# GpSimd makes the third shifted pattern of VectorE's packs in a gated attention kernel; 127 packs instead of 120

## The chip, the cores and the metric

The kernel runs on one core of a Trainium2 chip. The core has five engines with a queue each: TensorE (PE, with its weight loads shown as PEld), VectorE (DVE), ScalarE (ACT), GpSimd (POOL) and SyncE (SP, which here only starts DMAs). A queue is worked in order; semaphores tie the queues together. The metric is the device time of one execution in microseconds, as the median of several runs.

## What is computed

Two attention branches read the same `x` (2,048 tokens of 512) and are mixed by a gate of one number per token:

```
g = sigmoid((x * gate_w).sum(-1))
a: qkv = x @ A_wqkv;  p = softmax(q k^T * 16**-0.5);  a = (p v) @ A_wo      32 heads of 16
b: qkv = x @ B_wqkv;  pq = q w_phi;  pk = k w_phi
   phi_q = [softmax(pq), softmax(-pq)];  phi_k = [softmax(pk), softmax(-pk)]
   kv = phi_k^T v;  z = sum phi_k;  b = (phi_q kv / (phi_q z + 1e-6)) @ B_wo
out = g * a + (1 - g) * b
```

Nearly all the work is the softmax of branch a: 32 heads with 2,048 x 2,048 scores each.

## The kernel before

**Tiles.** A *unit* is the score block of one head, 128 keys against 512 queries. Four heads side by side in TensorE's 32-row tiles make a *pack*; 16 packs (all the keys) make a *group* of four heads and 512 queries, and 32 groups make the 512 packs, or 2,048 units.

**Two ways through the exponential.** Most units go to ScalarE: `_qk` writes two or three units' scores to PSUM, alternately, in a ring of five banks, `_exp` (L1019) turns them into bf16 in the tile `ET`, and `_pv` (through `_values`, L1085) multiplies a pack by the values and adds into the group's bank. Each exponential waits for its scores; each score call waits for the last exponential but one. The packs listed in `AWAY`, five bits per group for the packs 1, 4, 7, 10 and 13, go to VectorE instead. `_vector_bits` writes the scores of one unit at a time into one of the three other PSUM banks (L971 in `_scores`), and VectorE scales and shifts them into 16-bit integers (L911, tile `va`) whose bits, read as bf16, are a rough power of two. `_vector_terms` makes three copies of them, shifted by 30, 62 and 95 (`SHIFTS`, L927, tile `vp`). The four patterns, the unshifted one among them, are multiplied by the values (for the two last ones by values scaled by 0.75, tile `vc`) and added up on TensorE in `_pv_terms`; their sum comes close to the exponential. Up to two packs of a group make a *turn*: the eight bits instructions fill one half of `va`, and each term instruction covers the whole turn, 4,096 elements in a partition, or 2,048 where the turn has one pack. There are two halves of `va`, used in turns, and one `vp` tile for each shift.

**After a group.** `_norm` turns the bank, divides by the sum, multiplies by the gate and sends the result through DMAs into `onTA`; `_out` multiplies by `A_wo`. Branch b (`_b_quad`, `_b_kv`, `_b_num`, `_b_out`) is spread over the run in between: its exponentials are ScalarE's (L1258), most of its element work is VectorE's (L1229 to L1286). POOL fills constants at the start and does little else.

**Order.** Nothing is ordered by hand. `Plan.op` records each operation with its engine, a cost in microseconds, what it reads and writes, and a due time in packs; `SHIFT` moves the due times of tagged operations. `Plan.order` then runs through the operations, always taking for the engine that is free first what is ready and due first, with the booked costs, and so writes down each engine's queue. `emit` puts these queues and their semaphore waits into the program. TensorE's queue also gets *fillers*: value matmuls with zero weights (`_fill`, L1092), where its recent use falls under a share.

Of the kernel before, what the change touches and what calls it, by code (L numbers as in the profile page):

```python
# [6 lines left out]
ACT = mybir.ActivationFunctionType  # L7
ALU = mybir.AluOpType
# [7 lines left out]
QCH = 512  # L16
# [27 lines left out]
class Op:  # L44
    def __init__(self, eng, fn, cost, name, prio, rel, kind, lat):
        self.eng, self.fn, self.cost, self.name = eng, fn, cost, name
        self.prio, self.rel, self.kind, self.lat = prio, rel, kind, lat
        self.deps = []
        self.users = []
        self.left = 0  # L50
        self.need = False
        self.acquire = None
        self.release = None
        self.sem = None
        self.start = self.end = None
        self.commit = None
        self.array = 0.0
        self.filler = 0
        self.slack = None
        self.fits = True  # L60
        self.pad = False
        self.tiles = []
        self.filled = 0
        self.tag = None

# [38 lines left out]
class Plan:  # L104
# [4 lines left out]
    LAT = {"PE": 0.20, "ACT": 0.17, "DVE": 0.12, "POOL": 0.12, "SP": 2.2}  # L109
# [3 lines left out]
    EVICT = 30.0  # L113
    COST, NEAR = 30.0, 0.05
# [11 lines left out]
    def op(self, eng, fn, cost, reads=(), writes=(), deps=(), name="", prio=0.0, rel=-99, kind="full",  # L126
           acquire=None, release=None, lat=None, array=None):
        o = Op(eng, fn, cost, name, prio, rel, kind, self.LAT[eng] if lat is None else lat)
        found = {}
# [36 lines left out]
    def order(self):  # L166
# [15 lines left out]
        recent = []  # L182
        queues = {e: [] for e in self.ENGS}
        left = len(self.ops)
        seq = {id(o): i for i, o in enumerate(self.ops)}
        while left:
            best = None
            for e in self.ENGS:
                found, limit = [], 1e9
                for o in avail[e]:  # L190
# [4 lines left out]
                    for d in o.deps:  # L195
                        r = d.end + (d.lat if d.eng != e or e == "SP" else 0.0 if e == "PE" else self.CHAIN)
                        if r > t:
                            t = r
                    if o.acquire is not None:
# [34 lines left out]
            o = pick[1]  # L234
# [27 lines left out]
            free[e] = array.seq if e == "PE" else o.end  # L262
            queues[e].append(o)
# [113 lines left out]
class _Kernel:  # L377
# [10 lines left out]
    TURN = 2.2  # L388
    LAST, RAMP, PART = 8.0, 48, 24
# [335 lines left out]
    def _gate(self):  # L725
# [44 lines left out]
    AWAY = (15, 5, 27, 26, 20, 27, 14, 28, 30, 13, 23, 31, 14, 14, 30, 31, 29, 14, 23, 7, 31, 27, 23, 23, 30, 31, 11, 27, 11, 31, 23, 31)  # L770

    SHIFT = (
        ("k5", -3), ("k4", -10), ("v1", -6.5), ("p30", -4.5), ("p13", 7), ("p22", 8.5), ("q1", 3.5), ("w0", -10),
        ("p18", -11.5), ("b1", -7.5), ("v2", -5), ("x1", -5), ("v4", 6), ("p21", -3), ("p2", 0.5), ("k1", -6),
        ("p26", 10.5), ("k6", 6), ("b4", -3), ("p0", 1), ("g1", -6), ("p38", -5), ("p31", 1), ("d0", -3.5), ("p34",
        -1), ("p32", -6), ("v9", 6.5), ("e2", 13.5), ("p47", 6), ("p75", 2.5), ("b93", 11.5), ("b77", 6.5), ("b90",
        8.5), ("a0", 7.5), ("p89", -3.5), ("g4", 10.5), ("x90", -5.5), ("p104", -12), ("p98", 2), ("e4", 2), ("q5",
        6.5), ("x138", -0.5), ("p126", 1.5), ("x141", 13.5), ("p137", -1), ("t125", 7), ("p113", 12), ("b138",
        -4.5), ("a4", -6), ("b154", -14), ("p112", 10), ("p152", 11), ("p144", -2.5), ("p171", 4), ("p159", -10),
        ("p168", 11.5), ("p163", -0.5), ("p162", -12.5), ("x177", -14), ("g11", 4.5), ("x199", 0.5), ("p184", 8),  # L780
        ("d12", -0.5), ("p210", -3.5), ("p254", -12), ("p240", -11), ("p245", -7.5), ("p236", -2), ("g14", 4.5),
        ("b257", -3), ("t257", -4), ("b279", 1), ("p256", 2), ("p255", -5.5), ("p270", 4), ("p258", -14), ("p284",
        -12.5), ("x257", 2.5), ("b301", -8.5), ("p286", 12), ("p287", 14), ("p291", -10), ("b311", -1.5), ("p307",
        10.5), ("p296", -10.5), ("p294", -4), ("p315", 11.5), ("p306", -13.5), ("t289", 4), ("p300", -0.5), ("p302",
        -0.5), ("o0", 7), ("p304", -4.5), ("p297", 4), ("p293", 11.5), ("b327", 8.5), ("h5", 6), ("n5", 3), ("p318",
        7), ("p332", 2), ("p331", 7), ("p338", 4), ("p341", 7.5), ("p363", 12.5), ("h8", 4), ("x372", 6), ("p367",
        -8), ("p386", -5), ("p396", 1), ("b397", 7), ("f3", 6), ("b404", -2), ("p409", -8), ("p392", 0.5), ("p400",
        14), ("p421", -1.5), ("b420", -2), ("o8", -5.5), ("p403", -2), ("p405", -1), ("p423", 13.5), ("p438", 1.5),
        ("h14", 8), ("p432", -1.5), ("h12", -6.5), ("x445", -1), ("g27", 8.5), ("b471", 12), ("x449", -1.5),
        ("p456", -2.5), ("t449", -10.5), ("p464", 14), ("p476", -6.5), ("p467", 3.5), ("t481", 7), ("p478", -5),  # L790
        ("p470", 3.5), ("p482", -2), ("x487", -4), ("o15", 3), ("p496", -1), ("g30", -1), ("x509", -4), ("g31", 12),
        ("p501", 12), ("p511", 0.5), ("v3", -9), ("t7", 4), ("p8", 12.5), ("e1", -1), ("v8", 8.5), ("p50", -4),
        ("p82", -6), ("d4", -3.5), ("p107", -8), ("d8", -11), ("p133", 8), ("p146", 11), ("q6", 12.5), ("b177",
        -14), ("p217", 2), ("g13", 3), ("p224", 2), ("x244", 9), ("h3", 2.5), ("b295", 13), ("g17", 11.5), ("b308",
        0.5), ("x308", 9), ("b337", -9), ("p344", 3), ("h4", 3.5), ("o7", 13), ("x407", 1), ("p399", -4), ("b407",
        -8), ("x420", 9), ("b452", 12.5), ("p443", 8), ("o13", -4.5), ("p502", 3), ("p14", 12), ("p3", 9), ("t1",
        -12.5), ("p25", 12), ("t17", -12), ("b33", 7), ("b7", -1.5), ("b17", -4), ("gate", -1.5), ("e0", 13.5),
        ("e3", 7.5), ("p44", 2.5), ("x42", 4.5), ("p85", 7.5), ("p73", -3), ("x93", -2.5), ("p78", 13.5), ("p95",
        7.5), ("p123", -14), ("b212", -6.5), ("e12", 1), ("p198", -7), ("x180", -6), ("p178", 8.5), ("e14", 5),
        ("p211", 8), ("p222", 6.5), ("p238", -5.5), ("p230", 6), ("p283", -11), ("p281", 13.5), ("x321", 3),  # L800
        ("t327", 0.5), ("p319", -1.5), ("x340", -1), ("p389", 11.5), ("n8", -6.5), ("b401", -1), ("t407", -12),
        ("q14", 1), ("b426", 2.5), ("x426", 4.5), ("p447", -6.5), ("h15", -7), ("p462", -0.5), ("x465", -9.5),
        ("b481", 10.5), ("t477", 6.5), ("n14", 4.5), ("x477", -7), ("b503", -3.5), ("p510", -2.5), ("x481", 1),
        ("p5", 9), ("p19", 13), ("v0", 3), ("k3", -8.5), ("w1", -1), ("b10", 4), ("p35", -1), ("p37", -5.5), ("p43",
        12.5), ("p69", 1), ("p67", 0.5), ("b84", -3), ("p96", 10), ("b103", 5), ("b119", 5), ("p131", -10.5),
        ("t177", -0.5), ("b180", 8.5), ("b186", -4), ("x189", 2), ("q7", 8.5), ("x212", -2), ("b244", -5), ("p235",
        -11.5), ("b282", -7.5), ("x301", 6.5), ("p299", -0.5), ("p290", 9.5), ("p312", 1), ("g19", 11.5), ("x337",
        -3), ("g20", -5), ("g22", 12), ("x388", 10.5), ("b394", -10.5), ("p384", -1), ("x394", 3.5), ("p395", -8),
        ("b388", -1), ("o9", 6), ("p437", -6.5), ("p451", -6), ("p473", -3), ("x493", 0.5), ("g29", 1.5), ("b500",
        -5), ("b487", 11.5), ("p492", -2.5), ("p504", 8), ("b468", 9.5), ("x500", 8), ("b23", 7.5), ("x10", -10),  # L810
        ("x17", -3), ("b45", -0.5), ("q2", 0.5), ("p488", -4), ("n7", 2), ("p446", 8), ("p450", 11.5), ("t433",
        -3.5), ("p57", 11), ("p56", -9), ("p63", 7), ("b81", 7.5), ("n11", 1.5), ("b449", 7), ("n13", 7), ("x497",
        -10), ("t417", 8), ("p110", 4), ("p102", 9.5), ("p114", 11.5), ("p143", -8.5), ("p134", -6.5), ("p142", -4),
        ("p153", -7), ("t145", -0.5), ("p412", -0.5), ("x145", 7.5), ("g28", 10.5), ("n15", 10.5), ("x154", -10),
        ("o12", -5), ("p494", -1.5), ("x173", 10), ("x218", 7.5), ("g12", 6), ("x228", -4.5), ("x231", -1.5),
        ("p239", 5), ("h2", -8), ("x247", -12), ("x263", -0.5), ("n2", 9), ("g15", -11), ("f1", 5.5), ("q10", 1),
        ("p316", 5.5), ("o2", -9.5), ("p313", 10.5), ("p310", 8.5), ("p309", -2), ("x324", -8.5), ("p325", 9),
        ("p320", -5), ("p345", 2), ("p339", 12), ("h6", 12.5), ("p379", 8.5), ("p378", -2), ("p382", 11), ("p53",
        4.5), ("p39", -2), ("x58", -7), ("g3", -3.5), ("k12", 1), ("q3", 4.5), ("p83", -12.5), ("p79", 6.5),
        ("x103", -2), ("p108", 1), ("p124", 2), ("p129", -1.5), ("p139", -3), ("e9", 14), ("p158", -8), ("p169",  # L820
        -1), ("p166", -2.5), ("p176", -13.5), ("p188", 1.5), ("p204", -8), ("p190", -4), ("p191", 6), ("x196", 2),
# [673 lines left out]
```

## Time and profile before

The median of three runs is 757.48 us (757.35 to 757.73). The profiled execution has a span of 755.7 us from its first to its last instruction.

| engine | busy us | share of the span | instructions |
|---|---|---|---|
| ScalarE (ACT) | 740.9 | 98% | 647 |
| VectorE (DVE) | 723.2 | 96% | 1126 |
| TensorE (PE) | 719.6 | 95% | 7307 |
| GpSimd (POOL) | 7.8 | 1% | 17 |

Busy is the time in which an engine has at least one instruction under way, so that neighbours which overlap in the record are not counted twice; a group's mean duration can therefore be longer than its share of the busy time. The idle time behind a group's bar is that of the engine just before these instructions, with what ended it. The granted TensorE clock is 1.000 over the whole span.

### The profile page before, as it was taken

Reading aid. Unit: us, or ns where it says so; the run is one execution under the profiler, and the core shown is the slowest. Engines: PE = TensorE matmul, PEld = TensorE weight load, DVE = VectorE, ACT = ScalarE, POOL = GpSimd, SP = SyncE. Lnnn points to the kernel's source line nnn. Section 1 sums busy time; section 2 is a strip of 40 time slices with the busy share of each in tenths; the row PEclk is TensorE's granted clock in tenths of the full one; section 3 lists DMA queues with packets and bytes.
Section 4 is the critical chain, followed back from the end, with each engine's and each line's share of the span. In section 5 each row is a group of like instructions: output and inputs, shape, how many; then the busy total and the mean of one; then the engine's idle time right before and its main releaser. Section 6 shows DMA issues by size and latency. Waiting matters only on the chain.

```text
span 755.7 us, 17044 instructions
## 1 busy us (share of the span) xinstructions
PE 719.6 (95%) x7307; PEld 232.0 (31%) x7368; DVE 723.2 (96%) x1126; ACT 740.9 (98%) x647; POOL 7.8 (1%) x17
## 2 busy tenths in 40 slices
PE   8999999999999999999999999999999999999997
PEld 3334233333322322223222323223222223322332
DVE  6989899979999999999999999999999999999997
ACT  5999999999999999999999999999999999999996
POOL 3000000000000000000000000000000000000000
PEclk9999999999999999999999999999999999999999
DMA  9300001000000010100103111310112201131010
GB/s 212 131 5 6 10 8 17 8 3 14 8 8 15 2 14 9 15 9 3 21 13 57 24 15 37 73 27 8 23 29 47 38 17 29 29 73 28 11 27 29
DMA packets 90027, 21.78 MB, mean 29 GB/s; under 512 B 82912, under 2 KB 89440, under 8 KB 89952
## 3 DMA queue, kind: packets, MB, share of 16 engines
q1 hardware_dynamic: 88224, 20.17, 13.2%
q8 instruction: 57, 0.93, 0.5%
q10 hardware_dynamic: 1728, 0.52, 0.3%
q14 instruction: 18, 0.15, 0.1%
HBM read 4.21 MB, written 2.10 MB: 8 GB/s over the span
## 4 chain that ended last, share of the span: by engine, by line
ACT 93%; PE 5%; DVE 1%; DMA 1%; issue 0%; DVEq 0%
ACT ET L1019 89%; ACT bq L1258 4%; PE ps L971 1%; PE ps L1085 1%; DMA xT<-in_A_x_dram 1%; PE ps L714 1%; PE ps L1388 0%; PE ps L1434 0%; PE ps L641 0%; DVE va L911 0%; PE ps L992 0%; DVE kT L664 0%; DVE qT L697 0%; ACT xT L1444 0%; DVE V L720 0%
## 5 line engine op out<-in xcount | busy, mean ns | idle before, releaser
L1019 ACT ACTIVATE ET<-ps 128x1536 bf16<-128x1536 f32 x627 | 713.3, 1383 | 5.6 <-PE ps L971 5.3
L971 PE MATMUL ps<-qT,kT 32*128 32x512 bf16 x2048 | 314.6, 384 | 14.2 <-ACT ET L1019 7.3
L911 DVE TENSOR_SCALAR va<-ps 128x512 uint16<-128x512 f32 x480 | 311.5, 680 | 12.0 <-PE ps L971 9.5
L927 DVE TENSOR_SCALAR vp<-va 128x4096 uint16<-128x4096 uint16 (+1 forms) x204 | 219.2, 1086 | 0.9 <-PE ps L1085 0.6
L971 PEld LDWEIGHTS ps<-qT,kT 32*128 32x128 bf16 x2048 | 82.2, 91 | 260.6 <-ACT ET L1019 158.0
L1085 PE MATMUL ps<-ET,V 128*32 128x512 bf16 x1568 | 150.2, 386 | 0.4 <-DVE T L1106 0.2
L1085 PE MATMUL ps<-vp,vc 128*32 128x512 bf16 x960 | 86.4, 384 | 1.0 <-DVE vp L927 1.0
L1092 PE MATMUL ps<-kT,zero 128*32 128x512 bf16 x744 | 63.3, 384 | 0.0
L1085 PEld LDWEIGHTS ps<-ET,V 128*32 128x32 bf16 x1568 | 39.2, 95 | 65.0 <-issue 50.4
L641 PE MATMUL ps<-WB,xT 128*128 128x512 bf16 x164 | 50.0, 383 | 5.6 <-issue 3.0
L1085 PE MATMUL ps<-vp,V 128*32 128x512 bf16 x480 | 46.9, 384 | 0.5 <-DVE vp L927 0.5
L1085 PE MATMUL ps<-va,V 128*32 128x512 bf16 x480 | 47.3, 384 | 0.0
L641 PE MATMUL ps<-xT,WA 128*128 128x512 bf16 (+1 forms) x114 | 33.2, 375 | 2.8 <-issue 1.6
L1085 PEld LDWEIGHTS ps<-vp,vc 128*32 128x32 bf16 x960 | 23.1, 95 | 37.1 <-issue 19.5
L1258 ACT ACTIVATE bq<-bq 128x2048 bf16<-128x2048 bf16 x16 | 32.3, 2034 | 0.0
L1229 DVE CAST bq<-ps 128x512 bf16<-128x512 f32 x32 | 21.7, 682 | 4.1 <-PE ps L641 4.0
L1106 DVE STREAM_TRANSPOSE T<-ps 128x512 f32<-128x512 f32 x32 | 22.6, 707 | 2.2 <-PE ps L1085 2.2
L1092 PEld LDWEIGHTS ps<-kT,zero 128*32 128x32 bf16 x744 | 16.0, 94 | 25.1 <-issue 22.2
L714 PE MATMUL ps<-WA,xT 128*128 128x128 bf16 x256 | 21.1, 220 | 0.8 <-DVE V L720 0.3
L1256 DVE TENSOR_TENSOR bq<-bq,btree 128x2048 bf16<-128x2048 bf16 x16 | 19.4, 1210 | 0.0
L641 PEld LDWEIGHTS ps<-WB,xT 128*128 128x128 bf16 x192 | 11.9, 97 | 23.6 <-issue 13.4
L714 PEld LDWEIGHTS ps<-WA,xT 128*128 128x128 bf16 x256 | 15.1, 98 | 10.4 <-issue 6.9
(83 smaller groups left out, 330.9 us busy)
## 6 DMA issues: line engine op xcount, KB each, us to landing
turned<-T SPq DMA_DIRECT2D x240, 8.0 KB, 1.8
qT<-qs SPq DMA_DIRECT2D x120, 16.0 KB, 1.8
WB<-in_B_wqkv_dram SPq DMA_DIRECT2D x1, 1536.0 KB, 8.0
out_dram<-WB SPq DMA_DIRECT2D x12, 128.0 KB, 1.7
WA<-in_A_wqkv_dram SPq DMA_DIRECT2D x3, 384.0 KB, 5.5
WoA<-in_A_wo_dram SPq DMA_DIRECT2D x1, 512.0 KB, 9.0
WoB<-in_B_wo_dram SPq DMA_DIRECT2D x1, 512.0 KB, 9.6
WA<-in_A_wqkv_dram ACTq DMA_DIRECT2D x3, 128.0 KB, 4.1
```

Source lines behind the costliest of these rows:

```text
L641: ins = e.matmul(self._bank(job)[:, 0:n], lhs(c), rhs(c), start=(c == 0), stop=(c == 3))
L714: ins = e.matmul(self._bank(job)[:, P * tt:P * tt + P], self.xT[:, c, QCH * j + TOK * tt:QCH * j + TOK * tt + TOK], self.WA[:, 2, c, P * c ...
L911: parts.append(op("DVE", lambda e, j=j, job=job: e.tensor_scalar(self.va[:, pair, side, j, :], self._bank(job), SCALE * LOG2E * 128.0, (12 ...
L927: self.plan.op("DVE", lambda e, k=k, shift=shift: e.tensor_scalar(flat(self.vp[:, k]), flat(self.va[:, pair]), float(shift), None, op0=ALU ...
L971: return e.matmul(out, self.kT[32 * i:32 * i + 32, cp, kt * TOK:(kt + 1) * TOK], self.qT[32 * i:32 * i + 32, s, :], start=True, stop=True, ...
L1019: o = plan.op("ACT", lambda e: e.activation(self.ET[:, a % NS:a % NS + n, :], self.ps[:, self._ring(a):self._ring(a) + n, :], ACT.Exp, sca ...
L1085: ins = e.matmul(self._bank(ot)[32 * i:32 * i + 32, :], V[:, v0:v0 + 32], tile(), start=(kt == 0), stop=(kt == self.NT - 1), tile_position ...
L1092: ins = e.matmul(self._bank(ot)[32 * i:32 * i + 32, :], self.zero[:], self.kT[:, 0, 0:QCH], start=False, stop=False, tile_position=(0, 32 ...
L1106: op("DVE", lambda e: e.transpose(T1[:, side].rearrange("p b s -> p (b s)"), src()), 0.635, deps=last, writes=[b_T1[side]], name="n_t1", p ...
L1229: [lambda e, b, k=k: e.tensor_copy(bq[:, k].rearrange("p (g s v) -> p g s v", g=8, s=2)[:, :, 0, :], b.rearrange("p (g v) -> p g v", g=8))],
L1256: run("b_sub", two(2048), lambda e, out=out, t=t: e.tensor_tensor(out, p, spread(t[:, :, 0], 32), ALU.subtract), at, [pos, tree[side]], [buf])
L1258: op("ACT", lambda e, side=side: e.activation(sides[side], sides[side], ACT.Exp, scale=1.0 - 2 * side), self.c_act(2048) + 0.04, reads=[bu ...
```

## The change

Six things are changed.

1. The third term (shift 95) of every turn is made by POOL, and in the first turn the second too. `_pool_term` makes one pack of it in two instructions of 1,024 elements (`CHUNKS = 2`). Each waits for its two bits instructions, and for the value matmuls that read this part of `vp` before.
2. `vp`'s buffers are kept for each side of a turn, not for the whole turn.
3. The plan knows a port: an operation on POOL, or one of VectorE's whose name is in `PORT`, is not set to start before the last such operation has ended.
4. `AWAY` lists 127 packs instead of 120, at other places.
5. `SHIFT`, the list of moves of due times, is another one throughout.
6. The first value matmul of a group is ordered behind the last score matmul that VectorE's packs of the group before asked for (`asked`); both are TensorE's.

```diff
+    PORT = frozenset(("v_term", "vcopy", "b_max", "b_sub", "b_sum", "b_ratio", "b_mul", "kvbd", "n_den", "n_mul"))
...
-    LAT = {"PE": 0.20, "ACT": 0.17, "DVE": 0.12, "POOL": 0.12, "SP": 2.2}
+    LAT = {"PE": 0.20, "ACT": 0.17, "DVE": 0.12, "POOL": 0.15, "SP": 2.2}
...
+        o.port = eng == "POOL" or name in self.PORT
...
+                    if o.port and port > t:
+                        t = port
...
+            if o.port:
+                port = max(port, o.end)
...
+    EVERY, CHUNKS = 1000, 2
...
-    AWAY = (15, 5, 27, 26, 20, 27, 14, 28, 30, 13, 23, 31, 14, 14, 30, 31, 29, 14, 23, 7, 31, 27, 23, 23, 30, 31, 11, 27, 11, 31, 23, 31)
+    AWAY = (7, 21, 27, 7, 11, 25, 27, 15, 30, 31, 31, 15, 14, 15, 21, 31, 23, 29, 29, 14, 31, 31, 29, 15, 29, 31, 29, 31, 11, 31, 28, 31)
...
+            self.asked[pack // self.NT] = m
...
-    def _vector_terms(self, pair, packs):
-
-        size = len(packs)
+    def _vector_terms(self, turn, packs):
+
+        size, pair = len(packs), turn % 2
...
         for k, (shift, scaled) in enumerate(SHIFTS):
+            if k == 2 or k == 1 and turn % self.EVERY == 0:
+                for j, pack in enumerate(packs):
+                    b = self.b_vp[k][j]
+                    self._pool_term(pair, j, k, shift, b, packs[0] + self.TERM)
+                    self.terms[pack].append((lambda k=k, j=j: self.vp[:, k, j], b, scaled))
+                continue
             b = self.b_vp[k]
             self.plan.op("DVE", lambda e, k=k, shift=shift: e.tensor_scalar(
                 flat(self.vp[:, k]), flat(self.va[:, pair]), float(shift), None, op0=ALU.add),
-                         0.07 + n * 0.00026, reads=self.b_va[pair][0:size], writes=[b], name="v_term",
+                         0.07 + n * 0.00026, reads=self.b_va[pair][0:size], writes=b[0:size], name="v_term",
                          prio=packs[0] + self.TERM)
...
+    def _pool_term(self, pair, j, k, shift, b, due):
+
+        n = self.NB // self.CHUNKS
+        parts, bits = [], self.b_va[pair][j]
+        for c in range(0, self.NB, n):
+            flat = [t[:, c:c + n].rearrange("p n q -> p (n q)") for t in (self.vp[:, k, j], self.va[:, pair, j])]
+            sink, src = Buf(), Buf()
+            src.writers = bits.writers[c:c + n]
+            o = self.plan.op("POOL", lambda e, flat=flat: e.tensor_scalar(
+                flat[0], flat[1], 1.0, float(shift), op0=ALU.mult, op1=ALU.add), 0.08 + n * QCH * 0.00102,
+                reads=[src], deps=b.readers or b.writers, writes=[sink], name="p_term", prio=due)
+            bits.readers.append(o)
+            parts.append(o)
+        b.writers, b.readers = parts, []
...
+        self.b_va, self.b_vp = [[Buf(), Buf()] for _ in range(2)], [[Buf(), Buf()] for _ in SHIFTS]
...
         if kt == 0:
             self.ot[g] = Job()
+            deps.append(self.asked.get(g - 1))
```

## The prediction

> **What bounds the kernel now.** I read four views in this order: the page's busy shares and chain, the groups of instructions by line and shape, the stretches of 50 us, and short timelines.
>
> ```profile
> span 755.7 us, 17044 instructions
> ...
> PE 719.6 (95%) x7307; PEld 232.0 (31%) x7368; DVE 723.2 (96%) x1126; ACT 740.9 (98%) x647; POOL 7.8 (1%) x17
> ...
> ACT 93%; PE 5%; DVE 1%; DMA 1%; issue 0%; DVEq 0%
> ```
>
> Three engines look full, but the chain that ended last is ScalarE's (ACT) for 93% of the span. GpSimd (POOL) does next to nothing.
>
> ```profile
> L1019 ACT ACTIVATE ET<-ps 128x1536 bf16<-128x1536 f32 x314 | 500.0, 1592 | 5.6 <-PE ps L971 5.3
> L1019 ACT ACTIVATE ET<-ps 128x1024 bf16<-128x1024 f32 x313 | 367.2, 1173 | 0.0
> ...
> L911 DVE TENSOR_SCALAR va<-ps 128x512 uint16<-128x512 f32 x480 | 311.5, 680 | 12.0 <-PE ps L971 9.5
> ...
> L927 DVE TENSOR_SCALAR vp<-va 128x4096 uint16<-128x4096 uint16 x156 | 187.2, 1212 | 0.9 <-PE ps L1085 0.6
> ...
> L927 DVE TENSOR_SCALAR vp<-va 128x2048 uint16<-128x2048 uint16 x48 | 32.3, 678 | 0.0
> ...
> L1092 PE MATMUL ps<-kT,zero 128*32 128x512 bf16 x744 | 63.3, 384 | 0.0
> ```
>
> In 627 exponentials ScalarE waited 5.6 us, and the waits put that in the first 14 us. The two shapes' times add to 867 us because neighbours overlap in the record; the page gives 713.3 us for both together. They cover 314*3+313*2 = 1,568 score blocks of 128x512, so a block costs ScalarE 713.3/1568 = 0.455 us. The other 480 blocks, 120 packs of four, go to VectorE (DVE): L911 makes bits, and L927 three shifted copies of them. The 744 matmuls against `zero` are fillers, work that the plan can leave out.
>
> ```profile
> 250.00:300.00 50.00, 47.21 (x510) 14.69 (x513) 47.58 (x67) 50.00 (x46) 0.00 (x0) 1.00 0.05 9
> ...
> 350.00:400.00 50.00, 47.35 (x502) 13.96 (x502) 50.00 (x78) 50.00 (x44) 0.00 (x0) 1.00 0.14 26
> ```
>
> The columns are the stretch, its length, then PE, weight loads, VectorE, ScalarE, POOL, the clock and DMA. ScalarE is busy all 50 us; VectorE may be just as full (second row) without ScalarE losing anything, so VectorE at 96% is still covered.
>
> ```profile
> 401.64 1.22 DVE L927 TENSOR_SCALAR vp<-va 128x4096 uint16<-128x4096 uint16 x1
> 402.77 1.28 DVE L911 TENSOR_SCALAR va<-ps 128x512 uint16<-128x512 f32 x2
> ...
> 4.52 1.80 POOL L594 MEMSET qT<- 128x2048 bf16 x1
> 6.27 0.10 POOL L565 MEMSET eps<- 128x1 f32 x1
> ...
> 18.83 1.18 POOL L574 TENSOR_TENSOR bq<-wphi,head 128x256 bf16<-128x256 bf16 x2 [11.75 <-DMA wphi<-in_B_w_phi_dram]
> 20.62 0.29 POOL L728 COPY bq<-gw 128x128 bf16<-128x128 bf16 x1 [0.61 <-DMA gw<-in_gate_w_dram]
> ```
>
> A term's start is 1.13 us before the next start, 0.08 less than its record; by the same 0.08 a bits instruction takes 0.60 us and a half-size term 0.60 us. These are the paces used below. POOL's last work ends at 20.9 us and VectorE's first term starts at 22.8 us, so this trace has no moment in which the two could disturb each other.
>
> **The change, part by part.** The list of packs holds 127 instead of 120, in 73 turns, 54 of two packs and 19 of one.
>
> *ScalarE.* 28 blocks leave it: 28*0.455 = **-12.7 us**. The 32.3 us of branch B's exponentials (L1258) stay.
>
> *VectorE.* Third terms go, and the first turn's second: 107 full and 38 half-size terms remain of 156 and 48, so 49*1.13 + 10*0.60 = -61.4 us. 28 more bits instructions bring +16.8 us. VectorE's work falls from 723.2 to 678.6 us. This gives the time nothing by itself; it opens 743.0-678.6 = 64 us in the new span.
>
> *TensorE.* Per added pack, four lone score matmuls and twelve more value matmuls. A score call of four takes 0.34 us on the short timelines and a value call of four 0.22 us; I price a lone score call at most like a whole one: 28*0.34 + 21*0.22 = 14.1 us, less eleven score calls for ScalarE (3.7 us), so at most +10.4 us. TensorE is idle for 36 us, and the fillers hold another 186*0.22 = 41 us. With the span 12.7 us shorter, 77-10.4-12.7 = 54 us is left: nothing on the path. Were no filler given up, 13 us of idle time would still cover it.
>
> *POOL.* Each third term becomes two instructions per pack of 1,024 elements, the first turn's second term too: 127*2+4 = 258. No row shows this operation. Lower bound: the MEMSET of 2,048 elements, 1.75 us to the next start, so 0.88 us for 1,024. Upper bound: the two-input multiply, 0.59 us for 256, so 2.36 us. In between, the one-input COPY: 0.29 us for 128, of which 0.10 us is fixed by the one-element MEMSETs, so 0.10+1024*0.19/128 = 1.62 us. The plan books 0.08+1024*0.00102 = 1.12 us. I take 1.12: the plan's costs for bits (0.601) and full terms (1.135) meet the traced paces within 0.01 us, and 1.12 lies between the MEMSET and the COPY, whose 128 elements with a broadcast are a poor guide to a long run. POOL then works 289 us (227 to 609) in a span of 743.
>
> *The shared port.* If a POOL instruction and a VectorE instruction of the plan's port list exclude each other, the port carries VectorE's 145 terms (107*1.13+38*0.60 = 144 us), branch B's and the norms' instructions on that list (81.5 us in L1247 to L1286, 17.7 us in the norms, `kvbd` and the value copies) and POOL's 289: 532 of 743 us. VectorE has 678.6-243 = 435 us of work off the port, above all bits from PSUM, to lay beside POOL's 289. In a group that sends all five packs away, ScalarE takes 44*0.455 = 20.0 us; VectorE needs 5*(2.40+1.13) = 17.7 us (20.5 before), POOL and port 5*(2.24+1.13) = 16.9 us. It fits, so I cost the port at nothing; its cover is the 64 us of VectorE, and without it each wait counts in full.
>
> [...]
>
> *The waits.* The value matmuls of a third term now wait for POOL. Behind them in TensorE's queue stand the next scores, for which ScalarE waits. A turn comes every 743/73 = 10.2 us and a full one needs 4*1.12 = 4.5 us of POOL, whose instruction starts after two bits instructions instead of a whole turn's eight. So the third term is there early, except perhaps in the first turn, where POOL has eight instructions (9.0 us): 0 to 1.1 us, one instruction late. I add 1.1 us. The finer buffers (a side of a turn each), `asked` (an order within TensorE alone) and the new shifts issue the same DMAs and add no instruction; 0 from -1 to +2 us, the size of ScalarE's waits at start (5.3 us) being all there is to win there.
>
> **Sum.** 755.7-12.7+1.1 = 744.1 us of span. The median, 757.48 us, is 1.8 us above the profiled span, so the forecast is **745.9 us**, its own range 743.5 to 750.
>
> **Rivals.**
>
> *Waits at the port eat the gain.* Port instructions on VectorE: 145 terms, 128 in branch B, 42 others, so 315. Did they arrive at random, they would meet POOL with a chance of 289/743 = 0.39 and wait half an instruction, 0.56 us: 315*0.39*0.56 = 69 us. VectorE's 678.6+69+8 us of idle time at the ends = 756 us of span, about **757 us**. For it: VectorE's queue is in order. Against: 435 us of port-free work; with half of the waits avoided VectorE stands at 713 of 743 us, 96% as now.
>
> *POOL's instruction is long: slower.* Place: the term loop on POOL, 258 times. At the COPY row's 1.62 us POOL holds the port for 418 us, random waits are 315*0.56*0.81 = 143 us, VectorE ends at 678.6+143+8 = 830 us; with half avoided at 758. Middle: **about 795 us**. At 2.36 us the port itself binds: 609+243+21 = 873 us. With half of the waits avoided it decides from about 1.6 us an instruction; at 1.12 us it does not. For it: the COPY and multiply rows. Against: the plan's other costs are true to the trace.
>
> *The third term is late on TensorE.* Every 0.1 us late in each of 127 packs takes back 12.7 us: **757 us**. For it: the waits of weight loads on L927 now are 11.4 us in 35 times, so TensorE does arrive early at times. Against: the 5.7 us left in each turn, and four terms to put in any order.
>
> **Numbers.** Forecast 0.67. Gain partly or wholly eaten by port or late terms 0.16, half of it still above 0.2% of gain. Slower by a long POOL instruction 0.13, by lost order (late terms beyond 0.1 us) 0.04. 0.2% of the time is 1.5 us, about what a measurement can tell from none. Faster 0.67+0.08 = 0.75, within 0.2% 0.08, slower 0.17. The range runs from 743.5 (no added wait, 1.3 us better) to 759 (the first and third rival in full), leaving out the 0.17 above and little below.
>
> **What would show it.** ScalarE: 616 exponentials of about 700.6 us, idle time still near 6 us after its start. VectorE: 145 terms and 508 bits; if port waits matter, records of L927's line longer than 1.22 us or idle time before them. POOL: 258 instructions, start-to-start 1.12 us where they stand in a row. TensorE: no wait on POOL's `vp` beyond a few us, fewer than 744 fillers. The forecast is wrong if ScalarE shows tens of idle microseconds, released by scores that stand behind a value matmul waiting for POOL, or if VectorE is at 99% with long terms.

## The result, and the profile after

The changed kernel takes **770.2 us** (767.95 to 771.11 in four runs) beside 757.61 us for the kernel before: a ratio of 1.0162, with a 95% interval of 1.0146 to 1.0179. It is slower by 12.6 us; 745.9 us was forecast. One run of one experiment below, 819.66 us with the third term alone on POOL, was in a slower state of the chip and is left out there.

Lines of the page of the changed kernel (span, busy shares, chain, then groups of instructions; L1058 is the old L1019 and its row holds both shapes, L929 is the old L911, L951 the old L927, L1010 the old L971, L1125 the old L1085; L966 is new):

```profile
span 767.8 us, 17118 instructions
...
PE 728.6 (95%) x7252; PEld 227.3 (30%) x7252; DVE 714.8 (93%) x1095; ACT 732.3 (95%) x636; POOL 326.6 (43%) x275
...
PE 49%; DVE 32%; ACT 16%; DMA 1%; issue 1%; DVEq 0%
...
L1058 ACT ACTIVATE ET<-ps 128x1536 bf16<-128x1536 f32 x616 | 702.4, 1327 | 20.6 <-PE ps L1010 19.3
L966 POOL TENSOR_SCALAR vp<-va 128x1024 uint16<-128x1024 uint16 x258 | 318.7, 1235 | 427.1 <-PE ps L1125 235.4
L929 DVE TENSOR_SCALAR va<-ps 128x512 uint16<-128x512 f32 x508 | 330.4, 681 | 26.3 <-PE ps L1010 22.9
...
L951 DVE TENSOR_SCALAR vp<-va 128x4096 uint16<-128x4096 uint16 (+1 forms) x145 | 167.9, 1164 | 0.5 <-PE ps L1125 0.2
...
L1298 ACT ACTIVATE bq<-bq 128x2048 bf16<-128x2048 bf16 x16 | 31.2, 1958 | 5.8 <-DVE bq L1296 5.8
```

ScalarE and VectorE are less full than before (95 and 93% where they had 98 and 96), TensorE is as full as it was, and the chain is no longer ScalarE's. ScalarE did get its 11 fewer exponentials. But it now stands idle for 20.6 us ahead of exponentials and 5.8 us ahead of branch b's; less the one wait of 5.0 us before the first, 21.4 us lie inside its run, where the kernel before had 0.6.

The timeline shows one of the places (columns: start, duration, engine, line, operation, tiles, count; in brackets the idle time before and what ended it):

```profile
285.40 2.60 DVE L929 TENSOR_SCALAR va<-ps 128x512 uint16<-128x512 f32 x4
287.91 0.69 DVE L1305 TENSOR_TENSOR btree<-btree 128x512 f16<-128x512 f16 x1
288.53 2.06 DVE L951 TENSOR_SCALAR vp<-va 128x4096 uint16<-128x4096 uint16 x1
290.51 1.25 DVE L1307 TENSOR_TENSOR bsum<-btree 128x256 f32<-128x256 f16 x1
291.68 2.06 DVE L951 TENSOR_SCALAR vp<-va 128x4096 uint16<-128x4096 uint16 x1
...
286.17 6.49 POOL L966 TENSOR_SCALAR vp<-va 128x1024 uint16<-128x1024 uint16 x5 [1.58 <-DVE va L929]
...
285.64 7.07 ACT L1058 ACTIVATE ET<-ps 128x1536 bf16<-128x1536 f32 x6
294.88 1.45 ACT L1058 ACTIVATE ET<-ps 128x1536 bf16<-128x1536 f32 x1 [2.17 <-PE ps L1010]
...
293.80 0.38 PE L1010 MATMUL ps<-qT,kT 32*128 32x512 bf16 x1 [1.89 <-DVE vp L951]
```

The two full terms take 2.06 us, not 1.21, and the small sum between them 1.25, not 0.41: each is 0.84 us longer. At the same time five POOL instructions run as one piece of 6.49 us. TensorE waits 1.89 us for the second term with one score matmul of a later VectorE pack (its bits will overwrite the half of `va` that this term still reads), the scores of the next exponentials stand behind it, and ScalarE stops for 2.17 us. The plan's list has the term, the sum and the term ahead of the last three of these POOL instructions. The program has no semaphore by which POOL waits for them: those three started at 288.41, 289.59 and 291.56 us, ahead of the term at 288.53, the sum at 290.51 and the term at 291.68 us.

Over the run, by each queue's listed places and the traced starts, 32 of POOL's 258 instructions started ahead of at least one VectorE port instruction listed before them. Of the 315 VectorE instructions on the port list, 41 have records more than 0.2 us above their booked cost and the usual 0.08 us, 28.2 us together, none by more than 0.85 us; of the 780 others, one has.

TensorE's clock fell as well. Stretches of the changed kernel (stretch, length, PE, weight loads, VectorE, ScalarE, POOL, then the granted clock, a mean over the stretch, and the DMAs' share and GB/s):

```profile
192.00:196.00 4.00, 3.06 (x29) 0.63 (x26) 3.98 (x4) 2.55 (x2) 0.35 (x1) 0.57 0.02 4
...
295.00:299.00 4.00, 3.99 (x32) 0.77 (x28) 2.92 (x6) 3.21 (x3) 0.95 (x1) 0.57 0.00 0
356.00:364.00 8.00, 8.00 (x68) 1.66 (x56) 5.93 (x9) 6.00 (x6) 1.32 (x1) 0.57 0.01 3
489.00:497.00 8.00, 7.34 (x23) 1.59 (x23) 7.71 (x11) 5.70 (x5) 2.09 (x2) 0.57 0.05 16
```

Four times, each within about 1.2 us of the end of a stall of TensorE, the clock is halved, for 3.4 or 6.8 us and 23.9 us in all (0.57 is a stretch that is at half clock for most of its length); TensorE is then busy almost without a break, the first stretch apart, and ScalarE waits for it. In the kernel before the clock was 1.0 until the end.

### The profile page after: what moved, and what is told of

Its sections match the earlier page's. It is cut to its first block, busy times and chain, and to the rows that moved or that the text cites. A ratio compares the mean times of both kernels' runs of the same rounds, so it can differ in the third digit from the quotient of the medians.

```text
span 767.8 us, 17118 instructions
## 1 busy us (share of the span) xinstructions
PE 728.6 (95%) x7252; PEld 227.3 (30%) x7252; DVE 714.8 (93%) x1095; ACT 732.3 (95%) x636; POOL 326.6 (43%) x275
## 3 DMA queue, kind: packets, MB, share of 16 engines
q1 hardware_dynamic: 88224, 20.17, 13.7%
## 4 chain that ended last, share of the span: by engine, by line
PE 49%; DVE 32%; ACT 16%; DMA 1%; issue 1%; DVEq 0%
PE ps L1010 18%; PE ps L1125 17%; ACT ET L1058 16%; DVE va L929 12%; DVE vp L951 7%; PE ps L650 6%; DVE btree L1287 3%; DVE bq L1296 3%; PE ps L1132 2%; PE ps L723 2%; PE ps L1428 1%; DVE T L1146 1%; PE ps L1474 1%; DVE bq L1269 1%; DVE nb L1410 1%
## 5 line engine op out<-in xcount | busy, mean ns | idle before, releaser
L1058 ACT ACTIVATE ET<-ps 128x1536 bf16<-128x1536 f32 x616 | 702.4, 1327 | 20.6 <-PE ps L1010 19.3
L966 POOL TENSOR_SCALAR vp<-va 128x1024 uint16<-128x1024 uint16 x258 | 318.7, 1235 | 427.1 <-PE ps L1125 235.4
L929 DVE TENSOR_SCALAR va<-ps 128x512 uint16<-128x512 f32 x508 | 330.4, 681 | 26.3 <-PE ps L1010 22.9
L1010 PE MATMUL ps<-qT,kT 32*128 32x512 bf16 x2048 | 312.9, 388 | 19.6 <-ACT ET L1058 6.3
L951 DVE TENSOR_SCALAR vp<-va 128x4096 uint16<-128x4096 uint16 (+1 forms) x145 | 167.9, 1164 | 0.5 <-PE ps L1125 0.2
L1010 PEld LDWEIGHTS ps<-qT,kT 32*128 32x128 bf16 x2048 | 80.4, 91 | 271.8 <-ACT ET L1058 137.1
L1125 PE MATMUL ps<-ET,V 128*32 128x512 bf16 x1540 | 149.6, 388 | 0.2 <-DVE bq L1269 0.2
L1125 PE MATMUL ps<-vp,vc 128*32 128x512 bf16 x1016 | 92.7, 392 | 2.6 <-DVE vp L951 2.5
L650 PE MATMUL ps<-WB,xT 128*128 128x512 bf16 x192 | 56.5, 383 | 1.8 <-DVE T L1146 1.0
L1125 PEld LDWEIGHTS ps<-ET,V 128*32 128x32 bf16 x1540 | 38.9, 95 | 64.6 <-issue 50.6
L1125 PE MATMUL ps<-vp,V 128*32 128x512 bf16 x508 | 49.4, 390 | 5.7 <-DVE vp L951 5.5
L1125 PE MATMUL ps<-va,V 128*32 128x512 bf16 x508 | 50.3, 387 | 0.0
L1132 PE MATMUL ps<-kT,zero 128*32 128x512 bf16 x540 | 48.3, 396 | 0.0
L1125 PEld LDWEIGHTS ps<-vp,vc 128*32 128x32 bf16 x1016 | 24.2, 96 | 39.8 <-issue 25.9
L1296 DVE TENSOR_TENSOR bq<-bq,btree 128x2048 bf16<-128x2048 bf16 x16 | 22.9, 1430 | 0.0
L1428 PE MATMUL ps<-WoB,WT 128*128 128x512 bf16 x64 | 20.4, 398 | 1.2 <-DVE va L929 1.1
L1125 PEld LDWEIGHTS ps<-vp,V 128*32 128x32 bf16 x508 | 12.9, 96 | 24.3 <-DVE vp L951 10.6
```

Source lines behind the costliest of these rows:

```text
L650: ins = e.matmul(self._bank(job)[:, 0:n], lhs(c), rhs(c), start=(c == 0), stop=(c == 3))
L929: parts.append(op("DVE", lambda e, j=j, job=job: e.tensor_scalar(self.va[:, pair, side, j, :], self._bank(job), SCALE * LOG2E * 128.0, (12 ...
L951: self.plan.op("DVE", lambda e, k=k, shift=shift: e.tensor_scalar(flat(self.vp[:, k]), flat(self.va[:, pair]), float(shift), None, op0=ALU ...
L966: o = self.plan.op("POOL", lambda e, flat=flat: e.tensor_scalar(flat[0], flat[1], 1.0, float(shift), op0=ALU.mult, op1=ALU.add), 0.08 + n ...
L1010: return e.matmul(out, self.kT[32 * i:32 * i + 32, cp, kt * TOK:(kt + 1) * TOK], self.qT[32 * i:32 * i + 32, s, :], start=True, stop=True, ...
L1058: o = plan.op("ACT", lambda e: e.activation(self.ET[:, a % NS:a % NS + n, :], self.ps[:, self._ring(a):self._ring(a) + n, :], ACT.Exp, sca ...
```

## The experiments

Theory A is the one just told: POOL gets the port ahead of its listed turn, and VectorE's waits come where TensorE needs the result. Rival B: the load on the port costs this, whatever the order. Rival C: TensorE has no room for 127 packs. The first four kernels keep the changed kernel's queues for every engine, operation by operation; the third adds one POOL instruction at the start.

**POOL keeps the list.** Each POOL instruction waits for the VectorE port instruction that the list has last before it.

```diff
+        held = {}
...
             if o.port:
                 port = max(port, o.end)
+                other = held.get("DVE" if o.eng == "POOL" else "POOL")
+                if o.eng in ("POOL",) and other is not None:
+                    o.deps.append(other)
+                held[o.eng] = o
```

> Theory A, lost order: on the chip 32 of POOL's 258 instructions start ahead of VectorE port instructions that the list has before them, and VectorE then waits 0.84 us at a time. With each POOL instruction waiting for the VectorE port instruction listed before it, and every queue in the same order as in the changed kernel, the time falls to 745 to 750 us, VectorE's long records (2.05 us terms) go, ScalarE's idle time between its first and last exponential falls from 21 us to under 5, and the clock stays at 1.0. Rival B, the port's load: 258 POOL instructions of about 1 us on a shared port cost this whatever their order: 765 us or more. Rival C, too little room on TensorE for 127 packs: 765 us or more, with the half-clock stretches still there.

Measured: **744.9 us** (744.5 to 745.69), a ratio of 0.9828 (0.9813 to 0.9842) to the kernel before. From its groups:

```profile
L1063 ACT ACTIVATE ET<-ps 128x1536 bf16<-128x1536 f32 x308 | 485.1, 1575 | 6.2 <-PE ps L1015 5.7 <-PE ps L1130 0.2
L1063 ACT ACTIVATE ET<-ps 128x1024 bf16<-128x1024 f32 x308 | 355.8, 1155 | 0.0
...
L971 POOL TENSOR_SCALAR vp<-va 128x1024 uint16<-128x1024 uint16 x258 | 270.0, 1046 | 451.1 <-DVE vp L956 138.4 <-PE ps L1130 128.4 <-DVE va L934 97.8
...
L956 DVE TENSOR_SCALAR vp<-va 128x4096 uint16<-128x4096 uint16 x107 | 132.6, 1247 | 0.2
```

And the place shown above, in its timeline:

```profile
282.45 1.21 DVE L956 TENSOR_SCALAR vp<-va 128x4096 uint16<-128x4096 uint16 x1
283.59 0.41 DVE L1312 TENSOR_TENSOR bsum<-btree 128x256 f32<-128x256 f16 x1
283.93 1.21 DVE L956 TENSOR_SCALAR vp<-va 128x4096 uint16<-128x4096 uint16 x1
...
285.22 3.29 POOL L971 TENSOR_SCALAR vp<-va 128x1024 uint16<-128x1024 uint16 x3 [2.96 <-DVE vp L956]
```

Term, sum and term run at 1.21, 0.41 and 1.21 us, and POOL's three instructions come behind them, held 2.96 us for the term. The same 258 POOL instructions now have a mean of 1,046 ns, not 1,235. VectorE's long records on the port fall from 41 (28.2 us) to 15 (6.4 us); ScalarE's idle time inside its run is 1.4 us; the clock stays at 1.0 until the end. Theory A's numbers came in, but for the time, 0.1 us under its range, and for the long records, which did not all go. B and C, which asked for 765 us or more, fall: load and TensorE's list are the same.

**Both keep the list.** The same line with `("POOL", "DVE")`.

> As the first run, and VectorE's port instructions wait for the POOL instruction listed before them too. Theory A: within 3 us of the first run, 745 to 752 us; longer than it if VectorE now stands behind late POOL instructions. Rivals B and C: 765 us or more.

Measured: 748.9 us (747.79 to 750.54), ratio 0.9881 (0.9866 to 0.9896). In range, and 4 us more than with POOL waiting alone. No VectorE record on the port is long any more, but its terms now stand idle for POOL at their semaphores (waits by the profile: us in total, times, the longest), and the clock was halved twice, 6.8 us in all.

```profile
DVE vp L956 <- POOL vp L971: 8.8, 17, 1.0
```

Here it was better to make only the engine with time to spare wait.

**Short POOL instructions.** Each POOL instruction makes 64 of its 1,024 elements, so this kernel leaves most of the third term out; the rest of the tile is zero from the start.

```diff
...
-                flat[0], flat[1], 1.0, float(shift), op0=ALU.mult, op1=ALU.add), 0.08 + n * QCH * 0.00102,
+                flat[0][:, 0:64], flat[1][:, 0:64], 1.0, float(shift), op0=ALU.mult, op1=ALU.add), 0.08 + n * QCH * 0.00102,
...
```

> Each POOL term instruction handles 64 of its 1,024 elements (the rest of the tile is zero from the start, so the third term is left out for most of the data), so that POOL holds the port for about 0.1 us; all queues else as in the changed kernel. Theory A and rival B: no wait is left to speak of, 744 to 748 us, clock 1.0. Rival C, TensorE without room: 765 us or more, as TensorE's work is unchanged.

Measured: 747.53 us (745.5 to 750.84), ratio 0.9865 (0.9838 to 0.9893). No VectorE instruction waits at the port. Yet the median is 2.6 us above that of the first kernel, and in the profiled run, the slowest of the four, three stretches at half clock (13.7 us in all) remain. Its four runs go with the clock: mean clocks of 0.990, 0.995, 0.998 and 1.000 beside 750.84, 748.08, 746.99 and 745.5 us. So C was not empty: the new list has thin places on TensorE near 340, 395 and 477 us, where the clock fell in this run without any wait at the port. Why it falls there in one run and not in the next, or in the profiled run of the first kernel, which is thin at 340 and 393 us too, stays open.

**Halves.** Each POOL instruction is issued as two of 512 elements.

```diff
-            o = self.plan.op("POOL", lambda e, flat=flat: e.tensor_scalar(
-                flat[0], flat[1], 1.0, float(shift), op0=ALU.mult, op1=ALU.add), 0.08 + n * QCH * 0.00102,
+            o = self.plan.op("POOL", [lambda e, flat=flat, h=h: e.tensor_scalar(
+                flat[0][:, h:h + 512], flat[1][:, h:h + 512], 1.0, float(shift), op0=ALU.mult, op1=ALU.add)
+                for h in (0, 512)], 0.08 + n * QCH * 0.00102,
```

> Each POOL term instruction is issued as two of 512 elements one behind the other, queues as in the changed kernel. If VectorE gets the port between two POOL instructions, a wait shrinks from 0.84 to about 0.3 us. Theory A: about half of the 25 us lost against the forecast comes back, 753 to 762 us. If the port passed on only when POOL's queue is empty, or by rival B (total load, which grows a little by the added instructions): 768 us or more. Rival C: 768 us or more.

Measured: 766.49 us (765.29 to 768.05), ratio 1.0118 (1.01 to 1.0136): 3.7 us back, not the 8 to 17 expected. The longest port wait did shrink, to 0.44 us, so VectorE got the port between two POOL instructions. But there are 57 waits instead of 41, 22.1 us instead of 28.2. The expectation counted the waits as fixed in number. Two halves busy POOL longer than one whole (0.62 us each, undisturbed, against 1.045), which may be why there are more; that was not tested.

**Fillers at the stalls.** Fillers of four zero matmuls each are put into TensorE's queue ahead of the instructions at which the changed kernel's trace shows it standing still for anything but ScalarE. The page counts 280 more weight loads than the changed kernel's, so 70 of the 81 fillers went in; at the other places the value bank was changing.

```diff
...
+            if n and before is after:
+                out.append(Op("PE", [lambda e, ot=before: self._fill(e, ot)] * n, 0.0, "busy", 0.0, -99, "col", 0.2))
+            out.append(o)
...
```

(`n` is 2 to 13 at twenty places of the queue, by the length of the stall, and 0 elsewhere; `before` and `after` are the value banks in use on both sides.)

> The changed kernel with 81 more zero fillers put into TensorE's queue just ahead of the twenty instructions at which it stood still for 0.7 us or more (other than for ScalarE); POOL and VectorE as in the changed kernel. It asks how much of the loss is the halved clock and not the waits themselves. Theory A1, the clock is a part: the half-clock stretches (24 us in the profile) mostly go, VectorE's 0.85 us waits stay, and 6 to 10 us come back: 760 to 764 us. Theory A2, the clock only follows the stalls and costs nothing of its own: 768 to 771 us. Rival C, TensorE without room: more work on it, 772 us or more.

Measured: 765.22 us (765.09 to 765.49), ratio 1.01 (1.0085 to 1.0115). VectorE's port waits are the same (41, 28.3 us), the time at half clock falls from 23.9 to 6.8 us, and 5.0 us come back: a little under the 6 to 10 expected. The halved clock is thus some 5 us of the loss by this test, perhaps 2 more with the 6.8 us that remained (an estimate in proportion); by difference, most of the loss is the waits themselves.

**The third term alone on POOL.** The kernel before, with its 120 packs and its listed order; after the listing the third terms are moved to POOL's queue, in four instructions of 1,024 elements for a turn of two packs.

```diff
...
+        for o in moved:
+            o.eng, o.fn = "POOL", o.parts
+        q["POOL"] = sorted(q["POOL"] + moved, key=lambda o: o.start)
```

> The kernel before, with its 120 packs and its order, and only the third terms moved from VectorE's queue to POOL's, four instructions of 1,024 elements for a turn of two packs. VectorE loses 69 us of work, ScalarE none. Theory A: ScalarE bounds it as before, so nothing is won; where POOL starts ahead of VectorE's port instructions, waits of 0.85 us come up here too, and the third term takes 4.2 us where it took 1.14: 757 to 768 us, ScalarE's idle time up with the waits. Rival B, the port's load (250 us of POOL): the same loss as the changed kernel has against its forecast, 780 us.

Measured: 808.79 us (806.04 to 816.02), ratio 1.0656 (1.0634 to 1.0678), far above the 757 to 768 expected and above B's 780. ScalarE waits 48.6 us for scores, and TensorE's weight loads 17.0 us for POOL's term. The load on POOL is smaller than in the first kernel (240 instructions against 258) and the time 64 us longer, so the load alone does not set the time. It is no clean part of the change: the list knows nothing of POOL's 4.2 us a turn. Its trace shows both late third terms and port waits (VectorE's long records are 43 us, against 28 in the changed kernel), and the clock was halved for 51 us; what each of them costs was not told apart.

**The third term back on VectorE.** The changed kernel's 127 packs and its order, with the 258 instructions in VectorE's queue where the list has them on POOL, each written as one addition like VectorE's own terms.

```diff
...
+        for o in moved:
+            o.eng = "DVE"
+        q["DVE"] = sorted(q["DVE"] + moved, key=lambda o: o.start)
```

> The changed kernel's 127 packs and its order, with the 258 third-term instructions put into VectorE's queue at the places that the list gives them on POOL: no POOL, no shared port, 258 more VectorE instructions of 1,024 elements, about 0.34 us each by the 0.07 + n*0.00026 that the full terms keep to, 88 us. Theory A: VectorE then has 678.6 + 88 = 767 us of work and is the bound, 770 to 785 us, ScalarE's idle time well above the changed kernel's; POOL is what makes room for 127 packs. Rival D, the offload buys nothing and only the new order matters: 745 to 755 us.

Measured: 801.59 us (800.24 to 803.07), ratio 1.0581 (1.0563 to 1.0599). Its page:

```profile
PE 754.6 (95%) x7252; PEld 229.4 (29%) x7252; DVE 762.6 (96%) x1353; ACT 743.9 (93%) x636; POOL 7.8 (1%) x17
```

VectorE's work is the 767 us that were worked out, within 5, and D's 745 to 755 us are out: with 763 us of work on VectorE, 127 packs can't reach the forecast without POOL. The time is 17 us above the range. The added instructions stand in VectorE's queue in an order that was written for two engines, and the clock was halved for 41 us in all; which of the two made the 17 us was not tested.

## Why the prediction was wrong

**The step that failed** is the one on the shared port: "It fits, so I cost the port at nothing; its cover is the 64 us of VectorE, and without it each wait counts in full." The sums behind it hold: POOL's instruction, the load, and VectorE's work (689.2 us where no record is long, in the kernel in which both keep the list, against 678.6 worked out). But a sum says that an order without waits exists, not that the chip keeps it. Nothing in the change tied the order of the two queues on the port to the list. And the cover was taken as one pot of 64 us for the whole run, where a wait is covered only by what slack its own result has left: VectorE is idle for 53 us of the changed kernel's span, and ScalarE still lost 20.

**What it cost.** The changed kernel's span is 24.6 us above that of the kernel in which POOL keeps the list. ScalarE's idle time inside its run is 20.0 us of it (21.4 against 1.4), and its busy time 4.2 us (732.3 against 728.1), seen where an exponential starts after a pause and no longer overlaps the one before (in the changed kernel one of 128x1536 then takes 1.45 us alone, and in a row 1.34 us beyond the end of the one before). Of this, about 5 us are the halved clock, by the filler test; the rest, by difference, is VectorE's port waits carried through TensorE to ScalarE.

**The other steps** held, which the kernel that keeps the list shows, at 744.9 us against the forecast of 745.9:

- *ScalarE, -12.7 us:* its 616 exponentials take 699.7 us where 700.6 were forecast, with 6.2 us of idle time before them against 5.6.
- *POOL, 1.12 us an instruction:* the undisturbed record is 1.045 us, and three in a row take 3.29 us, so (3.29-1.04)/2 = 1.12 us from start to start, as booked; the slow rival (1.6 us and more) was not it. The plan's figure was the better guide than the COPY row.
- *TensorE, nothing on the path:* right for the sum, but thin places were left, at which the run with short POOL instructions was at half clock for 13.7 us.
- *Late third terms, 0 to 1.1 us:* TensorE's weight loads wait 1.1 us in all for POOL's term in the changed kernel. What came late were VectorE's own terms and branch b's instructions. So neither sign of being wrong came as written: ScalarE did show 21 idle us, but behind TensorE's waits for VectorE, and VectorE had long terms at 93%, not 99%.

**The rivals.** "Waits at the port eat the gain" named the mechanism and gave it 757 us. Its random meetings asked for 69 us of waits, and half of that avoided was to be free. There were 28 us, less than half, and the span is 24.6 us above the kernel with 6.4 us of them, the halved clock included: they come in rows (four between 186 and 193 us, three between 288 and 293 us). That a late VectorE leaves the port open to POOL's next instructions too would explain the rows; it was not tried by itself. The range ended at 759 us because that rival was priced by averages.

That POOL's instructions and those of VectorE's port list exclude each other was only an *if* in the prediction. The traces of this case show such waits: in the changed kernel terms and two-input instructions have records up to 0.85 us longer than usual, a little less than POOL's 1.045, and with both engines kept to the list no VectorE record on the port is long. The 508 bits instructions, which read PSUM, take 0.69 us at most in the changed kernel, as in the kernel before.

## What to carry to other kernels

An order worked out ahead over several engines was not kept here where no semaphore made it hold: the port, which two queues shared without one, was taken ahead of the listed turn 32 times. Where a plan relies on the turn, let the engine with time to spare wait for the listed instruction of the other: here one dependency turned 770.2 us into 744.9, and a second one, by which the busy engine waits too, gave 748.9. And price a wait by the slack of the result that it delays, not by the engine's idle time over the run.

## What the runs showed of the hardware

- VectorE and POOL took turns at the port, instruction by instruction: in the changed kernel, between 289.5 and 293.8 us, their records end at 289.51 (POOL), 290.59 (VectorE), 291.49 (POOL), 291.76 (VectorE), 292.66 (POOL) and 293.74 us (VectorE). With several POOL instructions at hand, no VectorE port instruction waited longer than for one of them (0.85 us at most with those of 1,024 elements, 0.44 us with halves).
- A short stall of TensorE had a price of its own. At 188.7 us it stood still for 2.79 us, and the clock was halved from 192.6 to 199.4 us; with fillers at the stalls the time at half clock fell from 23.9 to 6.8 us, and 5.0 us came back. The halved stretches inside the changed kernel's run are 3.4 us long once and 6.8 us three times. In the 3.4 us ahead of their four falls TensorE's records cover 1.09 to 1.70 us, and in the kernel in which both keep the list a fall at 390.4 us follows 3.4 us with 3.21 us covered. What makes the clock fall was not shown.
- POOL's `tensor_scalar` on 16-bit integers has undisturbed records of 1.045 us for 1,024 elements in a partition, 0.62 us for 512 and 0.24 us for 64. From these, an estimate: about 0.83 ns an element and 0.2 us for each instruction.
